# Attention and a two-layer ELU network on one core: the last 40 keys by 64x64 tiles, and a plain second layer in one more group

## The chip, the cores and the metric

The kernel runs on one core of a Trainium2 chip. Its time is the device time of one execution in microseconds (us); the profile is of one such execution. TensorE is PE in the profile (its weight loads are PEld), VectorE is DVE, ScalarE is ACT, GpSimd is POOL, and SyncE is SP, which issues nearly all the transfers.

## The reference

Everything is float32. q, k and v are 4 x 8 x 768 x 64 (batch, heads, positions, width). A query sees the first 8 keys and the 96 keys that end with itself. Scores have a penalty that grows with distance, then a softmax:

```python
scores = q @ k.T / 8 - slope[h] * dist
scores = where((j < 8) | ((0 <= i - j) & (i - j < 96)), scores, -1e9)
a = softmax(scores);  attn = a @ v
x = attn.transpose(0, 2, 1, 3).reshape(3072, 512)
h = x @ w_in                      # 512 x 2048
out = where(h > 0, h, exp(min(h, 0)) - 1) @ w_out    # 2048 x 512
```

## The kernel before

**Groups.** The 3072 rows are 12 groups of 256 (two row tiles of 128), numbered from 0. Each group has 4 pairs of heads for attention, then the two layers, over 16 blocks `fc` of 128 hidden units. A float32 factor is split into two float32r parts (HI and LO), and three of the four part products are summed. Groups 0 to 2 run interleaved, four blocks at a time (`SEGS`), while the 32 weight blocks are loaded and converted from 64-bit floats by ACT, DVE and POOL (`weight`); between segments their partial sums wait in the tiles `pa0` to `pa5` (`part`). The later groups run one after the other.

**Attention of groups 3 to 11.** `visit` number k is one run of TensorE work: the values product of the pair that was visited two before (`values`, line 616), then the scores of a new pair (line 469), in the same two PSUM banks. In between a pair goes through softmax on DVE and ACT (lines 457, 459), a division on POOL (579), a 32x32 transpose on DVE (584) into `tr`, a store to DRAM (`dd<-tr`, 593, two transfers) and a reload that completes the transposition (603): keys 0 to 127 into `pt`, and the last 40 keys into `pu`. `pu` is a constant pair of tiles in which one half of the 128 partitions stays zero; head pairs 0 and 2 use one half, 1 and 3 the other. `values` multiplies `pt` by `v` and `pu` by `u`, each with 8 matmuls in tiles of 128 rows x 64 columns and 64 moving columns; the trace has two records for each matmul. Scores have 8 matmuls in tiles of 64x64, with 168 moving columns. There are 36 pairs and 38 visits.

**Second layer.** `moe` (lines 834 and 860) is plain: per block 12 matmuls of 256 columns for the first layer and 6 of 512 for the second. `seven` (712 and 768) takes two blocks j = (2j, 2j+1) together with 7 products in place of 8: 24 matmuls up and 21 of 256 columns down. It needs sums of weights: `prepare(j)` forms four of them, splits each in HI and LO, stores three in DRAM (`mixed`) and writes the fourth over the right half of the weight block `w0`; each group reloads three per j into `mix` tiles, whose slots are `pa0` to `pa5` again. It also needs sums of activations (`combine`: lines 733 to 736 on DVE, two casts on ACT, two subtractions on DVE). Groups 0 to 2 use `moe`, 3 to 11 `seven` (`NE = 3`).

**Order.** Nothing is scheduled by hand: `Plan.order` simulates the engines with fixed costs, takes what is ready by due time, shares out slots, and writes one fixed order for each engine, SP's queue included. Tiles of one class get slots in the order in which they were asked for. `early` is a moment of the plan before which an operation isn't placed. Line 307 is the shared subtraction and line 299 the shared ACT copy, so they are told apart by tile names.

Of the kernel before, what the change touches and what calls it, by code (L numbers as in the profile page):

```python
# [244 lines left out]
class Kernel:  # L245
# [64 lines left out]
    def consts(self):  # L310
        self.ident = self.const("ident", [P, P])
        self.far0, self.far1 = self.const("far0", [P, LW]), self.const("far1", [P, LW])

        self.scale = self.const("scale", [P, self.NP])
        if self.ON_PE:
            self.minus1 = self.const("minus1", [P, P], F32R)
        self.pu = [self.const(f"pu{i}", [P, 4, 2, NT, 32]) for i in range(2)]
        self.nmax = self.const("nmax", [P, self.B * self.H * self.S // P])
        self.sums = {x: self.c.tile([P, 2 * NT, 4], F32, name=x) for x in self.SLOTS["st"]}

# [238 lines left out]
    def turned(self, b, hp, t0, ss, due, end, X, after):  # L559

        nc, p = self.nc, self.plan
        tr = self.sb("tr", "tr", [P, BLK, 2, NT, 32], slots=X.get("tr"))
        dd = self.dr("dd", "dd", [P * BLK, 2 * NT * 32])
        pt, pu = self.sb("pt4", "pt4", [P, 4, 2, NT, 32], slots=X.get("pt4")), self.pu[hp % 2]
        low = slice(HW, P) if hp % 2 == 0 else slice(0, HW)
        st = self.sum()
        prs = []
        for j in range(2):
            h, at = 2 * hp + j, due + 300 * j
            for i in range(NT):  # L570
                prs.append(self.sb("pr", "pr", [P, BLK * 32], slots=X.get("pr")))
                self.softmax(b, h, t0 + i, ss[j], i, prs[-1], 0, st, NT * j + i, at, after)
        self.inverse(st, 2 * NT, due - 3500, 500.0)
        for n, pr in enumerate(prs):
            j, i = n // NT, n % NT

            def divide(e, n=n, pr=pr):
                nc.gpsimd.memset(pr.t[:, LW:], 0.0)
                nc.gpsimd.tensor_scalar(pr.t[:, :LW], pr.t[:, :LW], st.t[:, n, 3:4], 1.0, ALU.mult, ALU.mult)  # L579

            p.add((("POOL", 160 + 1.1 * LW, True),), divide, [pr, st], [pr], due - 3000 + 10 * n)

            def turn(e, i=i, j=j, pr=pr):
                nc.vector.transpose(tr.t[:, :, j, i], pr.t.rearrange("p (b r) -> p b r", r=32))  # L584

            p.add((("DVE", 150 + 1.042 * 32 * BLK, False),), turn, [pr], [tr], due - 2500 + 10 * n, slack=300.0)
        outs = []
        for a, (w0, w1) in enumerate(((0, 4), (4, BLK))):
            w = w1 - w0
            at = slice(P * w0, P * w1)  # L590

            def out(e, w0=w0, w1=w1, w=w, at=at):
                nc.sync.dma_start(dd.t[at].rearrange("(p w) x -> p (w x)", w=w), tr.t[:, w0:w1].rearrange("p w j i r -> p (w j i r)"))

            outs.append(p.add(sp(), out, [tr], [dd], due - 2000, nbytes=P * w * 512, beside=tuple(outs)))
        for a, (w0, w1) in enumerate(((0, 4), (4, BLK))):
            w = w1 - w0
            rows = slice(0, P) if a == 0 else low
            at = slice(P * w0, P * w1)

            def back(e, x=(pt, pu)[a], w=w, rows=rows, at=at):
                src = dd.t[at].rearrange("(q k w) x -> (k w) q x", q=4, w=w)
                nc.sync.dma_start(x.t[rows].rearrange("k q j i t -> k q (j i t)"), src)

            p.add(sp(), back, [dd], [(pt, pu)[a]], due - 1900, nbytes=P * w * 512)
        return pt, pu

    def values(self, rest, hp, ss):

        pt, pu, v, u = rest  # L610
        v0, v1 = (x.t.rearrange("p (i r j d) -> p i r j d", i=NT, r=2, j=2) for x in (v, u))
        for a, vx, x in ((0, v0, pt), (1, v1, pu)):
            for i in range(NT):
                for r in range(2):
                    for j in range(2):
                        self.nc.tensor.matmul(ss[i].t[j * HW:(j + 1) * HW, r, LW:LW + HW].rearrange("p (c t) -> p c t", c=2), vx[:, i, r, j],  # L616
                                              x.t[:, 2 * r:2 * r + 2, j, i], start=(a, r) == (0, 0), stop=(a, r) == (1, 1))
# [40 lines left out]
    def prepare(self, j, due):  # L658
# [5 lines left out]
        p.add(sp(), lambda e: nc.sync.dma_start(kept.t, w0.t[:, :, right].bitcast(F32)), [w0], [kept], due, nbytes=P * M * 8)  # L664
        self.mixed[j] = {}

        def two(n):
            return dve(n) + pool(n)

        def split(tf, d):  # L670
            p.add(act(M) + pool(M, False), lambda e: self.copy(e, w0.t[:, HI, right], tf.t), [tf], [w0], d)
            p.add(two(M), lambda e: self.minus(e, w0.t[:, LO, right], tf.t, w0.t[:, HI, right]), [tf, w0], [w0], d + 10)

        def stored(n, tf, d):
            split(tf, d)
# [9 lines left out]
        def rest(a, ax, t, tf, d):  # L685
# [12 lines left out]
    def seven(self, rows, xh, xl, dues, step, last):  # L698

# [203 lines left out]
    def build(self):  # L903
# [58 lines left out]
        for x in self.pu:  # L962
            self.plan.add((("POOL", 620.0, True),), lambda e, x=x: self.nc.gpsimd.memset(x.t, 0.0), [], [x], 60000.0, early=50000.0)
# [260 lines left out]
def layouts(q, k, v, w_in, w_out):  # L1224
# [70 lines left out]
```

## Time and profile before

| | |
|---|---|
| Median of 3 runs | 677.93 us (676.97 to 679.39) |
| The profiled execution | 677.09 us, of which the span is 675.3 us |
| TensorE busy in the span | 646.4 us (96%) |
| DVE, ACT, POOL busy | 523.5, 425.5, 188.8 us |
| Granted TensorE clock, mean | 0.997 of 2.4 GHz |

The span runs from the first to the last instruction. The 1.8 us around it are not seen in the trace. A busy share is an average over the three stages that the windows tell apart: three interleaved groups with weight conversion up to about 222 us, the groups by `seven` from there to about 665 us, and the last stores.

### The profile page before, as it was taken

What the parts mean: (1) busy time and instruction counts of PE and PEld (TensorE: products, weight loads), DVE (VectorE), ACT (ScalarE), POOL (GpSimd) and SP (SyncE); (2) the same over time, 40 slices, a digit from 0 to 9 for tenths busy, and PEclk for the clock granted to TensorE, in tenths of its full rate; (3) what the DMA queues carried; (4) which work ended last, traced back from release to release, by engine and by line L of the source; (5) the groups of instructions that cost most, each with busy time, mean ns of one, the idle gap of its engine ahead of it and who ended that gap; (6) DMA issues with size and microseconds to landing.
All of it is one profiled execution on the core that took longest, in us unless ns stands there. A gap on an engine that the chain in (4) does not pass through costs nothing.

```text
span 675.3 us, 18188 instructions
## 1 busy us (share of the span) xinstructions
PE 646.4 (96%) x6534; PEld 594.4 (88%) x6534; DVE 523.5 (78%) x1709; ACT 425.5 (63%) x1217; POOL 188.8 (28%) x477
## 2 busy tenths in 40 slices
PE   8989999968989999999999999999999999999995
PEld 6767887757878899999999999999999999999995
DVE  6999998999976787777777777777777777766654
ACT  6998875556655556666666666666666666655552
POOL 3565575456563332112112112112111111110000
PEclk9999999999999999999999999999999999999998
DMA  8989735110177888788788888788788789775542
GB/s 316 359 303 401 278 120 157 49 62 32 63 228 218 272 279 247 255 261 272 233 265 252 245 263 263 242 265 272 234 266 259 236 261 275 218 228 151 172 141 81
DMA packets 104703, 151.85 MB, mean 225 GB/s; under 512 B 9248, under 2 KB 49952, under 8 KB 104608
## 3 DMA queue, kind: packets, MB, share of 16 engines
q1 hardware_dynamic: 104608, 150.64, 69.8%
q8 instruction: 53, 0.87, 0.5%
q14 instruction: 42, 0.34, 0.2%
HBM read 121.77 MB, written 28.84 MB: 223 GB/s over the span
## 4 chain that ended last, share of the span: by engine, by line
PE 76%; DVE 11%; DMA 5%; issue 2%; ACT 2%; POOL 2%; SPq 1%; DVEq 0%; ACTq 0%; POOLq 0%
PE h L712 27%; PE o L768 24%; PE o L860 5%; PE s L616 5%; PE h L834 5%; PE s L469 4%; DMA mixed<-w 2%; PE pv L502 1%; DVE g L393 1%; PE none L1057 1%; DVE g L395 1%; DVE gl L307 1%; DVE pr L457 1%; DVE w L307 1%; DMA pt<-dd 1%
## 5 line engine op out<-in xcount | busy, mean ns | idle before, releaser
L712 PE MATMUL h<-xh,w 128*128 128x256 f32 x1152 | 160.4, 281 | 1.1 <-DVE gg L722 1.1
L579 POOL TENSOR_SCALAR pr<-pr,st 128x168 f32<-128x168 f32 x144 | 64.6, 449 | 305.8 <-DVE st L477 292.8
L712 PEld LDWEIGHTS h<-xh,w 128*128 128x128 f32 x1152 | 145.3, 188 | 5.4 <-issue 3.3
L722 DVE SCALAR_TENSOR_TENSOR gg<-e,h 128x256 f32<-128x256 f32 x144 | 60.3, 419 | 84.8 <-ACT e L721 83.8
L720 ACT ACTIVATE e<-h 128x256 f32<-128x256 f32 x144 | 55.1, 383 | 75.5 <-PE h L712 75.3
L459 ACT ACTIVATE pr<-pr,nmax 128x168 f32<-128x168 f32 x192 | 82.4, 430 | 16.2 <-DVE nmax L457 15.7
L712 PE MATMUL h<-xl,w 128*128 128x256 f32 x576 | 91.2, 280 | 0.0
L712 PEld LDWEIGHTS h<-xl,w 128*128 128x128 f32 x576 | 77.8, 188 | 0.7 <-issue 0.5
L768 PE MATMUL o<-mix,sh 128*128 128x256 f32 x432 | 74.0, 279 | 0.0
L834 PEld LDWEIGHTS h<-xh,w 128*128 128x128 f32 x384 | 55.9, 188 | 17.5 <-DVE gl L307 9.1
L834 PE MATMUL h<-xh,w 128*128 128x256 f32 x384 | 61.6, 285 | 7.1 <-DVE gl L307 5.8
L457 DVE CUSTOM_DVE_ANT_0 pr<-s,far 128x168 f32<-128x168 f32 x192 | 54.3, 324 | 16.9 <-ACT xh L299 15.2
L860 PE MATMUL o<-w,gh 128*128 128x512 f32 x192 | 61.6, 405 | 3.8 <-DVE part L880 1.8
L299 ACT CAST sh<-sum 128x512 fp32r<-128x512 f32 x72 | 44.8, 622 | 31.9 <-DVE sum L736 31.9
L307 POOL TENSOR_TENSOR w<-g,w 128x256 fp32r<-128x256 f32 x64 | 55.0, 883 | 30.2 <-ACT w L299 24.4
L768 PE MATMUL o<-w,sh 128*128 128x256 f32 x432 | 62.6, 280 | 0.7 <-DVE ob L798 0.7
L721 ACT ACTIVATE e<-e 128x256 f32<-128x256 f32 x144 | 60.1, 417 | 4.1
L768 PEld LDWEIGHTS o<-mix,sh 128*128 128x128 f32 x432 | 61.0, 188 | 0.0
L768 PEld LDWEIGHTS o<-w,sh 128*128 128x128 f32 x432 | 56.0, 188 | 0.7 <-ACT e L720 0.7
L584 DVE STREAM_TRANSPOSE tr<-pr 128x192 f32<-128x192 f32 x144 | 49.1, 361 | 4.7 <-POOL pr L579 2.4
L307 DVE TENSOR_TENSOR sh<-sum,sh 128x512 fp32r<-128x512 f32 x72 | 49.3, 685 | 3.3 <-ACT sh L299 3.3
L299 ACT CAST rh<-gg 128x384 fp32r<-128x384 f32 x72 | 36.8, 511 | 21.8 <-DVE gg L722 21.2
(130 smaller groups left out, 1267.0 us busy)
## 6 DMA issues: line engine op xcount, KB each, us to landing
mix<-mixed SPq DMA_DIRECT2D x216, 256.0 KB, 4.1
qk<-in_qkv_dram SPq DMA_DIRECT2D x48, 312.0 KB, 3.4
v<-in_qkv_dram SPq DMA_DIRECT2D x48, 256.0 KB, 4.1
dd<-tr SPq DMA_DIRECT2D x36, 256.0 KB, 3.5
pt<-dd SPq DMA_DIRECT2D x36, 256.0 KB, 4.4
bits<-in_w_in_dram SPq DMA_DIRECT2D x16, 512.0 KB, 7.4
bits<-in_w_out_dram SPq DMA_DIRECT2D x16, 512.0 KB, 9.0
u<-in_qkv_dram SPq DMA_DIRECT2D x24, 256.0 KB, 4.8
```

The lines of the kernel that those rows point to most:

```text
L299: self.nc.scalar.copy(out, x)
L307: self.on(e).tensor_tensor(out, x, y, ALU.subtract)
L457: first = p.add((("DVE", 85 + 1.042 * LW, False),), lambda e: nc.vector.tensor_tensor_reduce(x(), s.t[:, i, :LW], tab, -(2.0 ** -(h + 1)), ...
L459: p.add(act(LW, extra=200), lambda e: nc.scalar.activation(x(), x(), AF.Exp, bias=nm, scale=-1.0, accum_out=st.t[:, n, 0:1]), [pr], [pr, s ...
L579: nc.gpsimd.tensor_scalar(pr.t[:, :LW], pr.t[:, :LW], st.t[:, n, 3:4], 1.0, ALU.mult, ALU.mult)
L712: nc.tensor.matmul(h.t, w1.t[:, s, cc * P:(cc + 1) * P], x.t[:, cc], start=n == 0 and s == HI and cc == 0, stop=n == 1 and cc == self.NCC - 1)
L720: p.add(act(W, True), lambda e: nc.scalar.activation(ex.t, h.t, AF.Relu, scale=-1.0), [h], [ex], d - 8000)
L721: p.add(act(W), lambda e: nc.scalar.activation(ex.t, ex.t, AF.Exp, scale=-1.0), [ex], [ex], d - 8000)
L722: p.add(dve(W), lambda e: nc.vector.scalar_tensor_tensor(gs(), ex.t, -1.0, h.t, ALU.add, ALU.max), [h, ex], [g], d - 8000)
L768: nc.tensor.matmul(acc[bank].t[:, half], a, b.t[:, LO if t == 1 else HI, x], start=j == 0 and t == 0 and n in first, stop=j == self.NFC // ...
L834: nc.tensor.matmul(h.t, w1.t[:, s, cc * P:(cc + 1) * P], x.t[:, cc], start=n == 0 and cc == 0, stop=n == 2 and cc == self.NCC - 1)
L860: nc.tensor.matmul(o.t[:, :at.stop - at.start], g.t[:, i * P:(i + 1) * P], w2.t[:, s, at], start=fc == f0 and n == 0 and s == HI, stop=fc ...
```

## The change

It has two parts.

**The last 40 keys.** `pu` holds one row tile in partitions 0 to 63 and the other in 64 to 127, without zeros, in two ordinary slots; `u` holds the values for both kinds of head pair. Its 8 matmuls become 8 of 64x64 tiles, four tiles in turn. `tr` and `pt` have the row tile ahead of the head, and `pu` is filled by two transfers (64 partitions, 256-byte pieces) where there was one (512-byte pieces).

**Group 3 by `moe`.** `SE = 4` is the first group by `seven`. `prepare` is planned beside group 3 rather than beside groups 0 to 2, not before 165 us of the plan; the three stored sums are split into `mix` tiles of their own rather than in place over `w0`, and only the fourth is written over `w0`. Slots are added: `gl` 3 (2 before), `tf` 4 (2), `hl` 2 (1).

```diff
-        self.pu = [self.const(f"pu{i}", [P, 4, 2, NT, 32]) for i in range(2)]
...
-        tr = self.sb("tr", "tr", [P, BLK, 2, NT, 32], slots=X.get("tr"))
+        tr = self.sb("tr", "tr", [P, BLK, NT, 2, 32], slots=X.get("tr"))
-        pt, pu = self.sb("pt4", "pt4", [P, 4, 2, NT, 32], slots=X.get("pt4")), self.pu[hp % 2]
-        low = slice(HW, P) if hp % 2 == 0 else slice(0, HW)
+        pt, pu = self.sb("pt4", "pt4", [P, 4, NT, 2, 32], slots=X.get("pt4")), self.sb("pu", "pu", [P, 4, 2, 32])
...
-            p.add(sp(), back, [dd], [(pt, pu)[a]], due - 1900, nbytes=P * w * 512)
+        p.add(sp(), back, [dd], [pt], due - 1900, nbytes=P * 2048)
+        backs = []
+        for i in range(NT):
+            def back(e, i=i):
+                src = dd.t[P * 4:].rearrange("(q k w) x -> (k w) q x", q=4, w=2)[:, :, i * HW:(i + 1) * HW]
+                nc.sync.dma_start(pu.t[i * HW:(i + 1) * HW].rearrange("k q j t -> k q (j t)"), src)
+
+            backs.append(p.add(sp(), back, [dd], [pu], due - 1890, nbytes=P * 512, beside=tuple(backs)))
...
+        for r in range(2):
+            for j in range(2):
+                for i in range(NT):
+                    rows = slice(i * HW, (i + 1) * HW)
+                    self.nc.tensor.matmul(out(i, r, j), ux[rows, hp % 2, r, j], pu.t[rows, 2 * r:2 * r + 2, j], start=False, stop=r == 1)
...
-            cost += 720.0
+            cost += 660.0
...
         def stored(n, tf, d):
-            split(tf, d)
+            x = self.sb("mix", "mix", [P, 2, M], F32R)
+            split(tf, x, left, d)
...
-        t1 = less(w0, right, w0, left, due)
-        t = less(w1, right, w0, right, due)
-        stored(3, t, due + 100)
-        rest(w1, right, t1, t, due + 200)
-        stored(2, t, due + 200)
-        rest(w1, left, t, t, due + 300)
-        stored(4, t, due + 300)
-        split(t1, due + 400)
+        t3, t1 = less(w1, right, w0, right, due), less(w0, right, w0, left, due + 50)
+        stored(3, t3, due + 100)
+        split(t1, w0, right, due + 200)
+        t2 = rest(w1, right, t1, due + 150)
+        stored(2, t2, due + 200)
+        stored(4, rest(w1, left, t2, due + 250), due + 300)
...
-                if n >= self.NE:
+                if n >= self.SE:
...
-            d = max(x[2 * j + 1] for (n, f0, f1), x in zip(segs, dues) if n < self.NE and 2 * j + 1 in x) + self.PREPARE[0]
-            todo.append((min(start[self.NE] - 1.0, d), lambda j=j, d=d: self.prepare(j, d)))
+            d = [x for (n, _, _), x in zip(segs, dues) if n == self.SE - 1][-1][2 * j + 1] + self.PREPARE[0]
+            todo.append((start[self.SE] - 1.0, lambda j=j, d=d: self.prepare(j, d)))
...
-    PREPARE = (9000.0,)
+    PREPARE, SE = (6000.0, 165000.0), 4
```

## Rows read from the trace of the kernel before

**Rows 1.** The page, busy us, share and instructions of each engine.

```profile
PE 646.4 (96%) x6534; PEld 594.4 (88%) x6534; DVE 523.5 (78%) x1709; ACT 425.5 (63%) x1217; POOL 188.8 (28%) x477
```

**Rows 2.** Windows: stretch, length, busy us of each engine, clock, DMA share, GB/s.

```profile
60.00:100.00 40.00, 40.00 (x362) 34.28 (x359) 37.41 (x93) 32.38 (x89) 25.63 (x38) 1.00 0.65 233
100.00:120.00 20.00, 18.89 (x149) 15.34 (x148) 18.23 (x46) 11.63 (x34) 11.80 (x21) 1.00 0.50 148
120.00:195.00 75.00, 65.81 (x438) 55.55 (x437) 73.62 (x163) 46.24 (x120) 44.16 (x59) 1.00 0.20 68
135.00:165.00 30.00, 21.93 (x128) 17.52 (x127) 29.27 (x54) 16.40 (x38) 17.37 (x21) 1.00 0.13 44
195.00:262.00 67.00, 62.97 (x667) 56.90 (x666) 48.65 (x168) 34.76 (x111) 24.23 (x69) 1.00 0.81 253
262.00:615.00 353.00, 352.59 (x3844) 340.51 (x3843) 257.67 (x932) 223.78 (x642) 51.64 (x216) 1.00 0.82 252
```

**Rows 3.** Waits of PE in 120 to 195 us, the longest: total, times, longest.

```profile
PE h L834 <- DVE gl L307: 4.9, 3, 3.4
```

**Rows 4.** DVE groups, 135 to 165 us: `prepare`, first and last of six.

```profile
L307 DVE TENSOR_TENSOR w<-tf,w 128x256 fp32r<-128x256 f32 x5 | 2.7, 532 | 0.0
...
L307 DVE TENSOR_TENSOR tf<-w,tf 128x256 f32<-128x256 f32 x2 | 0.8, 412 | 0.0
```

**Rows 5.** PE timeline of one visit: start us, length us, record counts.

```profile
347.89 0.69 PE L616 MATMUL s<-pt,v 128*64 128x64 f32 x16
348.41 0.64 PE L616 MATMUL s<-pu,u 128*64 128x64 f32 x16
348.98 0.80 PE L469 MATMUL s<-qk 64*64 64x168 f32 x16
349.71 0.74 PE L768 MATMUL o<-w,rh 128*128 128x256 f32 x4
```

**Rows 6.** PE group of the `pu` records, 262 to 615 us.

```profile
L616 PE MATMUL s<-pu,u 128*64 128x64 f32 x448 | 18.0, 223 | 0.0
```

**Rows 7.** Chain in order of time: start us, us, what.

```profile
121.11 1.17 PE o L860 x5
...
292.35 2.47 PE o L768 x21
```

**Rows 8.** SP timeline and PE timeline around the visit at 511 us.

```profile
505.37 0.58 SPq L603 DMA_DIRECT2D pu<-dd  x1
...
510.64 0.69 PE L616 MATMUL s<-pt,v 128*64 128x64 f32 x16
511.29 0.69 PE L616 MATMUL s<-pu,u 128*64 128x64 f32 x16
511.91 0.80 PE L469 MATMUL s<-qk 64*64 64x168 f32 x16
```

**Rows 9.** Tile `pu`: transfers to landing, all 36.

```profile
DMA to landing us min/median/max: 2.9/4.6/6.4
```

**Rows 10.** DVE groups, whole span: `prepare`, first and last of six.

```profile
L307 DVE TENSOR_TENSOR w<-tf,w 128x256 fp32r<-128x256 f32 x24 | 12.1, 502 | 6.7 <-POOL w L301 6.0 <-ACT w L299 0.7
...
L682 DVE TENSOR_TENSOR tf<-hl 128x256 f32<-128x256 f32 x10 | 5.8, 581 | 0.6 <-POOL w L307 0.6
```

**Rows 11.** DVE groups, whole span: what `combine` and the plain layer need.

```profile
L307 DVE TENSOR_TENSOR sh<-sum,sh 128x512 fp32r<-128x512 f32 x72 | 49.3, 685 | 3.3 <-ACT sh L299 3.3
L307 DVE TENSOR_TENSOR rl<-gg,rh 128x384 fp32r<-128x384 f32 x72 | 39.2, 544 | 1.2 <-ACT rh L299 1.2
L736 DVE TENSOR_TENSOR sum<-gg,sum 128x128 f32<-128x128 f32 x72 | 21.7, 301 | 2.5
L307 DVE TENSOR_TENSOR gl<-h,gh 128x256 fp32r<-128x256 f32 x48 | 19.9, 414 | 2.1 <-ACT gh L299 1.9
```

**Rows 12.** DVE groups, 195 to 262 us: `prepare`, first and last of six.

```profile
L307 DVE TENSOR_TENSOR w<-tf,w 128x256 fp32r<-128x256 f32 x6 | 2.5, 422 | 5.7 <-POOL w L301 5.7
...
L682 DVE TENSOR_TENSOR tf<-hl 128x256 f32<-128x256 f32 x1 | 0.5, 450 | 0.6 <-POOL w L307 0.6
```

More of the change, by code (lines that the diff above doesn't have):

```diff
@@ L583, in turn @@
             def turn(e, i=i, j=j, pr=pr):
-                nc.vector.transpose(tr.t[:, :, j, i], pr.t.rearrange("p (b r) -> p b r", r=32))
+                nc.vector.transpose(tr.t[:, :, i, j], pr.t.rearrange("p (b r) -> p b r", r=32))
             p.add((("DVE", 150 + 1.042 * 32 * BLK, False),), turn, [pr], [tr], due - 2500 + 10 * n, slack=300.0)
@@ L592, in out, with back @@
             def out(e, w0=w0, w1=w1, w=w, at=at):
-                nc.sync.dma_start(dd.t[at].rearrange("(p w) x -> p (w x)", w=w), tr.t[:, w0:w1].rearrange("p w j i r -> p (w j i r)"))
+                nc.sync.dma_start(dd.t[at].rearrange("(p w) x -> p (w x)", w=w), tr.t[:, w0:w1].rearrange("p w i j r -> p (w i j r)"))
             outs.append(p.add(sp(), out, [tr], [dd], due - 2000, nbytes=P * w * 512, beside=tuple(outs)))
[L596 to L603, printed above, removed]
-            p.add(sp(), back, [dd], [(pt, pu)[a]], due - 1900, nbytes=P * w * 512)
+        def back(e):
+            src = dd.t[:P * 4].rearrange("(q k w) x -> (k w) q x", q=4, w=4)
+            nc.sync.dma_start(pt.t.rearrange("k q i j t -> k q (i j t)"), src)
+        p.add(sp(), back, [dd], [pt], due - 1900, nbytes=P * 2048)
[5 more added lines that the diff above has]
+            backs.append(p.add(sp(), back, [dd], [pu], due - 1890, nbytes=P * 512, beside=tuple(backs)))
         return pt, pu
@@ L610, in values @@
         pt, pu, v, u = rest
[L611 to L617, printed above, removed]
+        vx = v.t.rearrange("p (i r j d) -> p i r j d", i=NT, r=2, j=2)
+        ux = u.t.rearrange("p (m r j d) -> p m r j d", m=2, r=2, j=2)
+        out = lambda i, r, j: ss[i].t[j * HW:(j + 1) * HW, r, LW:LW + HW].rearrange("p (c t) -> p c t", c=2)
+        for i in range(NT):
+            for r in range(2):
+                for j in range(2):
+                    self.nc.tensor.matmul(out(i, r, j), vx[:, i, r, j], pt.t[:, 2 * r:2 * r + 2, i, j], start=r == 0, stop=False)
+        for r in range(2):
+            for j in range(2):
+                for i in range(NT):
+                    rows = slice(i * HW, (i + 1) * HW)
+                    self.nc.tensor.matmul(out(i, r, j), ux[rows, hp % 2, r, j], pu.t[rows, 2 * r:2 * r + 2, j], start=False, stop=r == 1)
     def visit(self, k, due):
@@ L663, in prepare @@
         self.kept[j] = kept = self.dr(f"kept{j}", "kept", [P, 2, M])
-        p.add(sp(), lambda e: nc.sync.dma_start(kept.t, w0.t[:, :, right].bitcast(F32)), [w0], [kept], due, nbytes=P * M * 8)
+        p.add(sp(), lambda e: nc.sync.dma_start(kept.t, w0.t[:, :, right].bitcast(F32)), [w0], [kept], due, nbytes=P * M * 8, early=self.PREPARE[1])
         self.mixed[j] = {}
@@ L668, in two, with split @@
             return dve(n) + pool(n)
-        def split(tf, d):
-            p.add(act(M) + pool(M, False), lambda e: self.copy(e, w0.t[:, HI, right], tf.t), [tf], [w0], d)
-            p.add(two(M), lambda e: self.minus(e, w0.t[:, LO, right], tf.t, w0.t[:, HI, right]), [tf, w0], [w0], d + 10)
+        def split(tf, x, at, d):
+            p.add(act(M) + pool(M, False), lambda e: self.copy(e, x.t[:, HI, at], tf.t), [tf], [x], d)
+            p.add(two(M), lambda e: self.minus(e, x.t[:, LO, at], tf.t, x.t[:, HI, at]), [tf, x], [x], d + 10)
@@ L674, in stored @@
         def stored(n, tf, d):
-            split(tf, d)
+            x = self.sb("mix", "mix", [P, 2, M], F32R)
+            split(tf, x, left, d)
             s = self.mixed[j][n] = self.dr(f"mix{j}{n}", "mixed", [P, 2, M])
-            p.add(sp(), lambda e: nc.sync.dma_start(s.t, w0.t[:, :, right].bitcast(F32)), [w0], [s], d + 30, nbytes=P * M * 8)
+            p.add(sp(), lambda e: nc.sync.dma_start(s.t, x.t.bitcast(F32)), [x], [s], d + 30, nbytes=P * M * 8)
         def less(a, ax, b, bx, d):
@@ L680, in less, with rest @@
             hl, tf = self.sb("hl", "hl", [P, 2, M]), self.sb("tf", "tf", [P, M])
-            p.add(two(2 * M), lambda e: self.minus(e, hl.t, a.t[:, :, ax], b.t[:, :, bx]), [a, b], [hl], d)
+            p.add(two(2 * M), lambda e: self.minus(e, hl.t, a.t[:, :, ax], b.t[:, :, bx]), [a, b], [hl], d, early=self.PREPARE[1])
             p.add(two(M), lambda e: self.on(e).tensor_tensor(tf.t, hl.t[:, HI], hl.t[:, LO], ALU.add), [hl], [tf], d + 1)
             return tf
-        def rest(a, ax, t, tf, d):
+        def rest(a, ax, t, d):
+            tf = self.sb("tf", "tf", [P, M])
@@ L686, in rest @@
             p.add(two(M), lambda e: self.minus(e, tf.t, a.t[:, HI, ax], t.t), [a, t], [tf], d)
             p.add(two(M), lambda e: self.on(e).tensor_tensor(tf.t, tf.t, a.t[:, LO, ax], ALU.add), [a, tf], [tf], d + 1)
[L689 to L696 removed]
+            return tf
@@ L961, in build @@
         self.kept, self.mixed = {}, {}
-        for x in self.pu:
-            self.plan.add((("POOL", 620.0, True),), lambda e, x=x: self.nc.gpsimd.memset(x.t, 0.0), [], [x], 60000.0, early=50000.0)
         for j in range(NFC // 2):
-            d = max(x[2 * j + 1] for (n, f0, f1), x in zip(segs, dues) if n < self.NE and 2 * j + 1 in x) + self.PREPARE[0]
-            todo.append((min(start[self.NE] - 1.0, d), lambda j=j, d=d: self.prepare(j, d)))
+            d = [x for (n, _, _), x in zip(segs, dues) if n == self.SE - 1][-1][2 * j + 1] + self.PREPARE[0]
+            todo.append((start[self.SE] - 1.0, lambda j=j, d=d: self.prepare(j, d)))
         for _, f in sorted(todo, key=lambda x: x[0]):
@@ L996 @@
              "x": ["x0"], "xh": ["xh0", "xh1", "xh2"], "xl": ["xl0", "xl1", "xl2"], "e": ["e0", "e1"], "gh": ["gh0", "gh1", "gh2"],
-             "gl": ["gl0", "gl1"], "io": ["io0", "io1", "io2", "io3"], "part": [f"pa{i}" for i in range(6)], "mix": [f"pa{i}" for i in range(6)], "hl": ["x0"], "tf": ["tf0", "tf1"],
+             "gl": ["gl0", "gl1", "gl2"], "io": ["io0", "io1", "io2", "io3"], "part": [f"pa{i}" for i in range(6)], "mix": [f"pa{i}" for i in range(6)], "pu": ["pu0", "pu1"], "hl": ["x0", "ph2"], "tf": ["tf0", "tf1", "tf2", "tf3"],
              "g": ["io2", "io3"], "sum7": ["ph2", "x0"], "rh": ["gh0", "gh1"], "rl": ["gl0", "gl1"], "sh": ["xh2", "xl2"], "o2": ["v0"], "o3": ["t0"]}
@@ L1253, in layouts @@
     first = at % 4 * 32 + at // 4
-    vp = np.zeros_like(vv)
-    vp[..., 0, :, :, :, :] = vv[:, :, :, first, 0]
     key = at % 2 * 32 + at % HW // 2
+    vp = vv[..., :NT, :, :, :][:, :, :, first].copy()
+    vp[:, :, :, :, 0] = vv[:, :, :, first, 0]
     for m in range(2):
-        rows = slice((1 - m) * HW, (2 - m) * HW)
         x = np.zeros_like(vv[:, :, ::2, :HW, 1])
         x[:, :, :, :LW - P] = vv[:, :, ::2, (2 - m) * HW - (LW - P):(2 - m) * HW, 1]
-        vp[:, :, ::2, rows, 1] = x[:, :, :, key[:HW]]
+        x = x[:, :, :, key[:HW]]
+        for i in range(NT):
+            vp[:, :, ::2, i * HW:(i + 1) * HW, 1, m] = x[:, :, :, :, i]
     halves = lambda x: x.reshape(B, nb, H // 2, D, 2, -1).swapaxes(3, 4).reshape(B, nb, H // 2, 2 * D, -1)
```

## The prediction

> **What bounds the kernel now.** I read the page's busy line first: TensorE has 646.4 us of 675.3 busy [rows 1], so only two things can move the end, TensorE's work and its 29 us of idle time. The windows by stage then say where the idle time lies [rows 2]. From 262 to 615 us PE is busy for 352.59 of 353 us: there a microsecond of matmuls removed is a microsecond gained, and relief of any other engine is worth nothing. From 60 to 100 us it is busy throughout as well, with DVE at 37.41 of 40. But from 100 to 120 it idles 20 - 18.89 = 1.1 us and from 120 to 195 it idles 75 - 65.81 = 9.2 us, of which 8.1 lie in 135 to 165. DVE is busy there for 73.62 of 75 us. The DMA share of 0.20 excludes transfers as the limit. From 195 to 262 PE idles 4.0 us with DVE at 48.65 of 67 (73%).
>
> The waits name the engine of the middle stretch [rows 3]: the first layer's matmuls wait for `gl`, the last product of the DVE chain that frees the PSUM bank, for 4.9 us in three pieces. What keeps DVE from it: in 135 to 165 us, beside the conversion of weights, it makes the sums of `prepare`, six groups from 2.7 us down to 0.8, together 10.8 us of the 29.27 that it works there [rows 4].
>
> **The visits.** In one visit the 16 `pt` records take 348.41 - 347.89 = 0.52 us, the 16 `pu` records 0.57 and the 16 scores records 0.73 [rows 5]. Per record, scores have 168 columns and the others 64. In columns over time that is 1024 / 0.57 = 1.8 per ns with two tiles side by side and 2688 / 0.73 = 3.7 per ns with four. So the four tiles of 64x64 do stream together, and about twice as fast. The new `pu` block uses the same four tiles in the same turn. Its price lies between 0.57 us (if its records are bound by their number and not by their columns: 0.57 / 16 = 36 ns each, and scores' 46 ns each doesn't exclude that) and 1024 / 3.7 = 0.28. Some of each block is the change of tile shape ahead of the next, and one such change stays; a block that begins afresh, at 511.29, takes 0.62 instead of 0.57 [rows 8]. I allow 0.10 us for the change of shape, an estimate, and halve the remaining 0.47: 0.23 us saved per visit, ends 0 and 0.29. The number of changes of shape stays the same wherever scores follow the values: the change from 128x64 to 64x64 moves ahead of `pu`, and none is left ahead of scores.
>
> Behind 262 us, where PE is full, 448 `pu` records are 28 visits [rows 6]: 28 x 0.23 = 6.5 us (0 to 8.1). The other 8 of the 36 lie in stages with idle time; of their 1.9 us I count half, 0.9 (0 to 2.3).
>
> The Trainium skill (TensorEngine Tiling (Array Packing), Performance Considerations) speaks against this: a matmul has about 60 cycles of overhead, and no tiling factor is to be taken from a dimension that is already small, as 64 columns are. At 2.4 GHz 60 cycles are 25 ns, so 16 records would by it not go under 0.40 us, and the saving would be near 0.1 us in place of 0.23. No row of before shows it, since no block has four tiles and 64 columns.
>
> **The second transfer for `pu`.** SP issues `pu` in 0.58 us [rows 8]. A second issue moves what is queued behind it on SP (the next `u`, `v` and `mix` loads) by as much, and the second half lands some 0.6 us later than today's whole. SP mostly waits for PE in that stage, so its queue has room. The landing has little: issued at 505.37 with a median of 4.6 us to land and a maximum of 6.4 [rows 9], `pu` was just in time or late for 511.29. That block began 0.65 us after `pt` in place of 0.52, a wait of 0.13. If two visits of each of the 7 groups behind 262 lost the whole 0.6 us, it would cost 8.4 us; but the planner counts the second issue too and puts other matmuls ahead of a visit whose data it thinks late. I take 0.6 us in all, ends 0 and 8.4.
>
> **Group 3 by `moe`.** Behind the first stage PE's pace is its matmul rate. 5 records of 512 columns take 1.17 us, 21 of 256 columns 2.47 [rows 7]. Two blocks of the plain second layer are 12 records, 12 x 0.234 = 2.81 us, against 2.46 by `seven`: 0.35 more, eight times, +2.8 us. The first layer is the same in both. This is certain as long as PE is full.
>
> On DVE the group gets lighter. Beside the ELU, which both have, `seven` needs for two blocks `sh` 0.685, `rl` 0.544 and four sums of up to 0.30, together 2.4 us; the plain layer needs two `gl` of 0.414, 0.8 [rows 11]. Eight times 1.6 is 12.8 us less.
>
> **`prepare` moves.** All of it on DVE is 44.1 us in six groups from 12.1 down to 5.8 [rows 10]. 7.6 us of that lie in 195 to 262 already [rows 12], so up to 36 us leave the time before 195. With them gone, DVE's need in 120 to 195 falls well under PE's, conversion of the late weights ends earlier, and what is left is a stage like 60 to 100 us, in which PE lost nothing. Of the 10.3 us of idle time in 100 to 195 I leave 2: -8.3 us. Bounds: -10.3 (all of it), 0 (something else holds the weights, which no row suggests).
>
> The price is paid behind it. In the counterpart of 195 to 262 DVE's need becomes 48.65 - 7.6 - 12.8 + 44.1 = 72.4 us in 67 + 2.8, 104%. But the 44.1 were worked in a crowded stage: the costliest group has a mean of 0.502 us over the span [rows 10] and 0.422 in 195 to 262 [rows 12]. Scaled by 0.84 they are 37, and the sum is 65, 94%. POOL, at 24.23 of 67, can take some, and a little of `prepare` fits ahead of it. 94% with PE full is what 60 to 100 us shows; 98% with 12% of PE's time lost is what 120 to 195 shows. So the stretch's idle time may be 2 us or 8 instead of 4; I take 5, +1.0.
>
> A wait is added: the 24 stored sums take their `mix` slots ahead of group 4's first reload, since the class is served in order. Whatever `prepare` is late then holds PE at group 4's first second layer, at about 250 us, and everything behind it.
>
> **The sum.** -6.5 - 0.9 + 0.6 + 2.8 - 8.3 + 1.0 = -11.3 us on an execution of 677.1 us, so 665.8. The median shown is 0.8 above this execution; the prediction for a median is 666.6.
>
> **Rivals.**
> (1) The stall moves. DVE at 98% of the `prepare` stretch costs PE 12% of 67 us, 8.2 in place of 5, and some late weights still hold PE up (6 us left in place of 2): +7.2, 673.8. For it: 120 to 195. Against it: the third `gl` slot, and that the 12.8 us of `combine` are gone.
> (2) Four tiles don't pay at 64 columns, because each record has its price: -7.4 and no more, 674.0. For it: no row with this shape. Against it: scores at 3.7 columns per ns. This is the skill's rule driven to its end; by the rule itself, with 0.1 us left per visit, it would be 670.
> (3) Slower. `prepare` isn't through when group 4 needs its first sums. DVE's idle time in 195 to 262 is 18.4 us; with 12.8 + 7.6 released it is 38.8, 5.3 short of 44.1 without any help. If the durations are stretched by a third more, to 58, it is 20 short, and PE stands nearly that long at about 250 us. It decides from 13.4 us of lateness on; at 17 the time is 683. For it: the ordered slots, and that `part` holds them until groups 0 to 2 end. Against it: POOL's room, and lower clean durations.
> (4) The `pu` half lands too late in most visits, +6: 672.6. For it: the 0.13 us at 511.29. Against it: the planner's order.
>
> **How the numbers follow.** Main case 0.55 (662 to 671), (1) 0.17, (2) 0.08, (3) 0.10, (4) 0.10. The range takes the main case, and (1), (2) and (4) up to 674.5: 660 to 674.5, low end from the bounds -8.1, -1.5, +2.8, -10.3 and 0. A measurement here tells no less than 0.3% (2 us). Faster: all of the main case and nearly all of (1), (2) and (4), 0.86; same 0.04; slower 0.10.
>
> **What would show it.** `pu` records in tiles 64*64, with about 0.25 to 0.3 us to the scores, and visits near 1.58 us instead of 1.82. No `prepare` in DVE's groups before 150 us; PE full from 60 to about 185. Lines 834 and 860 in group 3, and no line 768 before about 250. DVE at about 90% from 185 to 250, and no wait of TensorE for `mix` at group 4's first second layer: that wait would make the forecast wrong. So would `pu` blocks of 0.4 us or more, or waits for `pu<-dd` in every group.

## The result, and the profile after

The changed kernel takes 659.45 us (median of 4 executions, 658.65 to 663.09) against 677.92 us for the kernel before beside it: a ratio of 0.9732 (95% interval 0.9696 to 0.9768), 18.5 us less. Timed once more it took 658.81 us (median of 5, 657.95 to 660.02), ratio 0.9726 (0.9697 to 0.9756). Forecast were 666.6 us, in a range of 660.0 to 674.5: the direction was right, the gain was 7 us too small.

The profiled execution was the slowest of the first four, 663.09 us with a span of 661.2. The busy line of its page, beside [rows 1]:

```profile
PE 641.3 (97%) x6462; PEld 587.2 (89%) x6462; DVE 504.0 (76%) x1658; ACT 419.0 (63%) x1211; POOL 199.0 (30%) x494
```

The same line of the second profiled execution, 658.23 us with a span of 656.4, which is nearer to the median:

```profile
PE 638.0 (97%) x6462; PEld 585.0 (89%) x6462; DVE 504.6 (77%) x1658; ACT 419.5 (64%) x1211; POOL 200.1 (30%) x494
```

From [rows 1] to this one TensorE's busy time falls by 646.4 - 638.0 = 8.4 us and its idle time by 28.9 - 18.4 = 10.5 us. The windows of the first profile, with the columns of [rows 2], say where:

```profile
60.00:100.00 40.00, 39.51 (x359) 33.57 (x358) 34.05 (x105) 33.19 (x98) 19.51 (x38) 1.00 0.62 219
100.00:120.00 20.00, 19.86 (x164) 17.30 (x163) 17.95 (x31) 12.43 (x30) 11.26 (x16) 1.00 0.36 115
120.00:195.00 75.00, 73.63 (x541) 64.70 (x540) 63.79 (x157) 46.29 (x127) 41.81 (x66) 1.00 0.22 70
135.00:165.00 30.00, 30.00 (x191) 26.52 (x190) 25.18 (x52) 18.95 (x44) 14.13 (x19) 1.00 0.03 10
195.00:262.00 67.00, 63.72 (x576) 54.16 (x575) 54.30 (x168) 36.43 (x121) 44.20 (x93) 0.97 0.71 233
262.00:615.00 353.00, 350.66 (x3870) 337.87 (x3869) 257.57 (x930) 223.07 (x637) 52.74 (x213) 1.00 0.81 247
```

In 120 to 195 us TensorE now idles for 1.4 us (9.2 before) and DVE works 63.79 of 75 (73.62 before). The 30 us that had 8.1 us of idle time are full. In 195 to 262 the idle time is 3.3 us (4.0 before), though the weight sums are made there now. The waits of TensorE in that stretch (total, times, longest):

```profile
PE o L866 <- ACT gh L299: 2.7, 2, 1.6
PE h L840 <- DVE gl L307: 0.6, 2, 0.4
```

TensorE waits nowhere for `mix`. The first product of `seven` (line 774 now) starts at 268.9 us. One visit in TensorE's timeline, beside [rows 5]:

```profile
369.29 0.69 PE L617 MATMUL s<-pt,v 128*64 128x64 f32 x16
369.90 0.46 PE L622 MATMUL s<-pu,u 64*64 64x64 f32 x16
370.19 0.75 PE L468 MATMUL s<-qk 64*64 64x168 f32 x16
370.87 0.50 PE L774 MATMUL o<-w,rh 128*128 128x256 f32 x2
```

From the start of one block to the next: `pt` 0.61 us (0.52 before), `pu` 0.29 (0.57), scores 0.68 (0.73), together 1.58 us instead of 1.82.

### The profile page after: what moved, and what is told of

The parts are those of the page before. It is cut to its first block, busy times and chain, and to the rows that moved or that the text cites. A ratio compares the mean times of both kernels' runs of the same rounds, so it can differ in the third digit from the quotient of the medians.

```text
span 661.2 us, 17979 instructions
## 1 busy us (share of the span) xinstructions
PE 641.3 (97%) x6462; PEld 587.2 (89%) x6462; DVE 504.0 (76%) x1658; ACT 419.0 (63%) x1211; POOL 199.0 (30%) x494
## 4 chain that ended last, share of the span: by engine, by line
PE 81%; DVE 10%; ACT 3%; POOL 3%; issue 2%; DMA 1%; SPq 0%; DVEq 0%; POOLq 0%; ACTq 0%
PE h L718 27%; PE o L774 23%; PE o L866 10%; PE h L840 9%; PE s L468 3%; PE s L617 3%; PE s L622 2%; PE none L1061 1%; DVE pr L456 1%; PE pv L501 1%; DMA pu<-dd 1%; ACT pr L458 1%; DVE g L394 1%; DVE gl L307 1%; PE t L521 1%
## 5 line engine op out<-in xcount | busy, mean ns | idle before, releaser
L728 DVE SCALAR_TENSOR_TENSOR gg<-e,h 128x256 f32<-128x256 f32 x128 | 53.6, 419 | 76.8 <-ACT e L727 76.0
L866 PE MATMUL o<-w,gh 128*128 128x512 f32 x256 | 82.5, 406 | 3.4 <-ACT gh L299 3.1
L718 PE MATMUL h<-xl,w 128*128 128x256 f32 x512 | 81.2, 280 | 0.0
L718 PEld LDWEIGHTS h<-xl,w 128*128 128x128 f32 x512 | 69.2, 188 | 0.9 <-issue 0.7
L456 DVE CUSTOM_DVE_ANT_0 pr<-s,far 128x168 f32<-128x168 f32 x192 | 54.3, 324 | 18.5 <-ACT xh L299 13.7
L774 PE MATMUL o<-mix,sh 128*128 128x256 f32 x384 | 65.8, 279 | 0.0
L774 PE MATMUL o<-w,sh 128*128 128x256 f32 x384 | 55.7, 280 | 0.7 <-DVE ob L804 0.7
L727 ACT ACTIVATE e<-e 128x256 f32<-128x256 f32 x128 | 53.4, 417 | 3.6
L866 PEld LDWEIGHTS o<-w,gh 128*128 128x128 f32 x256 | 43.7, 191 | 12.1 <-ACT gh L299 5.4
L774 PEld LDWEIGHTS o<-mix,sh 128*128 128x128 f32 x384 | 54.2, 189 | 0.0
L774 PEld LDWEIGHTS o<-w,sh 128*128 128x128 f32 x384 | 49.8, 189 | 0.7 <-ACT e L726 0.7
```

The lines of the kernel that those rows point to most:

```text
L456: first = p.add((("DVE", 85 + 1.042 * LW, False),), lambda e: nc.vector.tensor_tensor_reduce(x(), s.t[:, i, :LW], tab, -(2.0 ** -(h + 1)), ...
L718: nc.tensor.matmul(h.t, w1.t[:, s, cc * P:(cc + 1) * P], x.t[:, cc], start=n == 0 and s == HI and cc == 0, stop=n == 1 and cc == self.NCC - 1)
L727: p.add(act(W), lambda e: nc.scalar.activation(ex.t, ex.t, AF.Exp, scale=-1.0), [ex], [ex], d - 8000)
L728: p.add(dve(W), lambda e: nc.vector.scalar_tensor_tensor(gs(), ex.t, -1.0, h.t, ALU.add, ALU.max), [h, ex], [g], d - 8000)
L774: nc.tensor.matmul(acc[bank].t[:, half], a, b.t[:, LO if t == 1 else HI, x], start=j == 0 and t == 0 and n in first, stop=j == self.NFC // ...
L866: nc.tensor.matmul(o.t[:, :at.stop - at.start], g.t[:, i * P:(i + 1) * P], w2.t[:, s, at], start=fc == f0 and n == 0 and s == HI, stop=fc ...
```

## The experiments

**Each part by itself.** Two kernels, each with one half of the change: the tiles alone (the hunks of `turned`, `values` and the planner's cost 660, with the two `pu` slots), and the plain layer alone (`prepare` in its new form, `SE = 4`, and the slots of `gl`, `hl` and `tf`, with three of `tf`).

```diff
# tiles_only, on the kernel before
-        pt, pu = self.sb("pt4", "pt4", [P, 4, 2, NT, 32], slots=X.get("pt4")), self.pu[hp % 2]
+        pt, pu = self.sb("pt4", "pt4", [P, 4, NT, 2, 32], slots=X.get("pt4")), self.sb("pu", "pu", [P, 4, 2, 32])
...
# plain_only, on the kernel before
-                if n >= self.NE:
+                if n >= self.SE:
...
-    PREPARE = (9000.0,)
+    PREPARE, SE = (6000.0, 165000.0), 4
```

> Only the 64x64 tiles and the two transfers for pu; group 3 still by seven, sums where they were. My theory (the parts add up; 36 visits x 0.234 = 8.4 us of matmuls less, of which the 28 behind 262 us count in full, less some waiting for the later half of pu): 670 to 672.5. Rival (shorter visits relieve the first stage too, so this part carries the gain that my sum lacked): 662 to 666. Rival (the gain per visit is lost in waits): 676 to 678.

> Only group 3 by the plain layer with the sums moved beside it; pu is as before, and the scratch class tf has 3 slots and not 4, for room. My theory: 12 to 14 us less idle time ahead of 262 us, against 2.8 us more matmuls and a little idle time beside group 3: 665.5 to 669. Rival (the moved sums stall group 3 as much as they had stalled the first stage): 676 to 681. The parts add up if this gain and that of the tiles alone together make 18.5 us.

The tiles alone took 667.67 us, ratio 0.9858 (0.9825 to 0.9892), 9.6 us less than before. The plain layer alone took 667.09 us, 0.9848 (0.9818 to 0.9878), 10.2 less. The tiles alone took less than the 670 to 672.5 us that I expected and more than the first rival's 662 to 666; the plain layer came out as expected. The sum of the two is 19.8, the whole change gave 18.5: the parts add up within their intervals, so nothing shows that one lives on the other. The windows of the tiles alone, where the sums are still beside the first groups:

```profile
120.00:195.00 75.00, 66.94 (x423) 56.58 (x422) 70.54 (x151) 44.09 (x113) 40.99 (x56) 0.93 0.19 65
...
262.00:615.00 353.00, 353.00 (x3904) 340.98 (x3903) 262.32 (x947) 226.60 (x646) 51.63 (x216) 1.00 0.82 256
```

The first stage keeps 8.1 us of idle time (9.2 before), in an execution whose granted clock is 0.93 there and not 1.00, and the later stage is full with two transfers for `pu` in it. The plain layer alone fills the first stage and pays behind it:

```profile
120.00:195.00 75.00, 74.20 (x579) 65.43 (x578) 62.30 (x162) 44.76 (x125) 37.54 (x66) 1.00 0.26 84
195.00:262.00 67.00, 63.56 (x541) 54.47 (x541) 51.92 (x160) 36.18 (x120) 44.96 (x87) 1.00 0.64 209
```

**Why the `pu` block is short.** The program gives the two row halves in turn. If they stream together because of that, the two row tiles one after the other should cost about what two tiles did.

```diff
# rows_in_turn, on the changed kernel
-        for r in range(2):
-            for j in range(2):
-                for i in range(NT):
+        for i in range(NT):
+            for r in range(2):
+                for j in range(2):
```

> The changed kernel with the loop over the row tile outermost in the pu block: the same 16 records of 64x64 tiles, but only two tiles take turns at a time. If four tiles streaming together make the gain, the block goes back from 0.28 to 0.5 or more us, the visit from 1.58 to 1.81, and the time is 659.5 + 7.0 = 666.5 (665 to 668). If it is that half the rows are gone, or that each record has its price, the order doesn't matter: 659.5.

It took 659.55 us, ratio 0.9734 (0.9704 to 0.9765): the same as the changed kernel. TensorE's timeline of one of its visits:

```profile
365.86 0.69 PE L617 MATMUL s<-pt,v 128*64 128x64 f32 x16
366.47 0.47 PE L622 MATMUL s<-pu,u 64*64 64x64 f32 x16
366.76 0.77 PE L468 MATMUL s<-qk 64*64 64x168 f32 x16
367.45 0.50 PE L774 MATMUL o<-w,rh 128*128 128x256 f32 x2
```

The `pu` block is 0.29 us again. So my reason, the turn in the program's order, fell; the gain does not hang on it. The run would fit two other reasons: that both row halves are used in the block, or that 64 rows are cheaper than 128. The kernel before has blocks of the same shape on one row half alone, in the attention of group 2:

```profile
67.35 0.68 PE L502 MATMUL pv<-pt,u 64*64 64x64 f32 x16
67.97 0.73 PE L860 MATMUL o<-w,gh 128*128 128x512 f32 x2
```

There 16 records take 0.62 us with the change of shape behind them, so 64 rows alone do not make a block short, and the use of both halves is what stays. That is a comparison of two kinds of block and not of one edit; `pu` with both row tiles on one half was not tried.

**What the weight sums cost before.** The kernel before, and the changed kernel, with the sums left out: the same number of stores, of the weights as they are. The waits between the sums and their stores go with them.

```diff
# before_no_sums, on the kernel before; after_no_sums likewise on the changed one, with early=self.PREPARE[1]
-        t1 = less(w0, right, w0, left, due)
-        t = less(w1, right, w0, right, due)
-        stored(3, t, due + 100)
...
+        for n in (3, 2, 4):
+            s = self.mixed[j][n] = self.dr(f"mix{j}{n}", "mixed", [P, 2, M])
+            p.add(sp(), lambda e, s=s: nc.sync.dma_start(s.t, w1.t[:, :, right].bitcast(F32)), [w1], [s], due + 30 + 100 * n, nbytes=P * M * 8, early=100000.0)
```

> The kernel before, without the sums and splits of prepare: the three stored blocks are copies of a weight block as it is, with the same size and number of transfers, from 100 us of the plan on. My theory (DVE, crowded by prepare, held the first stage): PE's idle time in 100 to 195 us falls from 10.3 to under 2, and the time to 664.5 to 668. Rival (conversion of the late weights alone fills DVE, or their transfers): 10 us of idle time stay, 675 to 678.

> The changed kernel, without the sums and splits of prepare in the same way. It gives what the moved sums still cost beside group 3. My theory (DVE is at 81% there and POOL at 66%, and PE idled 3.3 us in 195 to 262 and 1.3 in 262 to 315): 655 to 657.5. Rival (they are hidden, and those waits are attention's): 658.5 to 660.

Without sums the kernel before took 658.95 us, ratio 0.9735 (0.97 to 0.9771): 18.1 us less, where the step of the forecast had at most 10.3, and below the 664.5 to 668 us that I expected of this run. The page's busy line of this kernel:

```profile
PE 642.0 (98%) x6534; PEld 595.5 (91%) x6534; DVE 488.5 (74%) x1646; ACT 417.4 (64%) x1194; POOL 154.7 (24%) x435
```

And three of its windows:

```profile
100.00:120.00 20.00, 20.00 (x164) 17.66 (x163) 17.30 (x37) 12.34 (x30) 11.34 (x22) 1.00 0.75 240
120.00:195.00 75.00, 74.25 (x580) 65.67 (x580) 54.04 (x142) 45.07 (x124) 27.93 (x54) 1.00 0.36 115
195.00:262.00 67.00, 67.00 (x705) 63.79 (x704) 50.41 (x178) 40.19 (x119) 11.99 (x44) 1.00 0.80 252
```

Two things are to be seen. The 4.0 us of idle time in 195 to 262 of before, which the forecast had kept, are gone too: they belonged to the sums. And the same 6534 records of TensorE are busy for 642.0 us instead of 646.4 [rows 1]. TensorE's work is the same, so 4.4 us of what looked like work were lost time. Idle time 28.9 to 15.0 is 13.9 us; 13.9 + 4.4 = 18.3 us agree with the 18.1 between the medians.

What this run does not tell apart is the arithmetic of the sums and their order. In the kernel before the four sums of one j are split in place over the right half of `w0`, one after the other, so that a split waits until the store ahead of it has landed; without sums these waits are gone too. In 195 to 262 us of the kernel before, POOL waits for such stores (total, times, longest):

```profile
POOL w L301 <- DMA mixed<-w: 18.2, 6, 4.6
```

In 120 to 195 us the same wait is 3.1 us, and DVE has only 1.4 us without work [rows 2], so there DVE's load is the nearer reason. For the 4.0 us behind 195 the wait in place is a rival that no run tests.

The changed kernel without sums took 666.54 us, ratio 0.9849 (0.9819 to 0.9878), 7 us more than with them. Its longest wait of TensorE (total, times, longest):

```profile
PE s L617 <- DMA pt<-dd: 11.1, 2, 10.4
```

Three rows of its SP timeline (start, length, what, how many):

```profile
188.62 1.37 SPq L591 DMA_DIRECT2D dd<-tr  x2
...
194.17 1.94 SPq L673 DMA_DIRECT2D mixed<-w  x3
...
203.38 0.43 SPq L596 DMA_DIRECT2D pt<-dd  x1
```

With no arithmetic to wait for, 19 of the 32 stores (24 `mixed`, and 8 `kept`, which save the right half of `w0`) were issued between 180 and 201 us of SP's queue, mostly at 0.5 to 0.7 us each. Ten of them, beside other transfers, stand between a pair's store to `dd` and its reload, and TensorE waited for `pt` for 10.4 us in one piece. Neither expectation held. The run says nothing of the sums beside group 3: it made a stall of its own. The next one takes its place.

**What the sums cost after.** The arithmetic of the sums is taken out, their stores stay at their places: two copies on ACT fill each tile that is stored.

```diff
# copies_for_sums, on the changed kernel
-        def split(tf, x, at, d):
-            p.add(act(M) + pool(M, False), lambda e: self.copy(e, x.t[:, HI, at], tf.t), [tf], [x], d)
-            p.add(two(M), lambda e: self.minus(e, x.t[:, LO, at], tf.t, x.t[:, HI, at]), [tf, x], [x], d + 10)
+        def split(x, at, d):
+            p.add(act(M), lambda e: self.copy(e, x.t[:, HI, at], w1.t[:, HI, right]), [w1], [x], d)
+            p.add(act(M), lambda e: self.copy(e, x.t[:, LO, at], w1.t[:, LO, right]), [w1], [x], d + 10)
```

> The changed kernel with the moved sums' VectorE and GpSimd work left out: each split is two copies of a weight block on ScalarE, stored through the same tiles at the same point of the plan, so that the transfers keep their pace. My theory (beside group 3 the sums crowd DVE, and PE still loses about 5 us there): idle time of PE in 195 to 262 us from 3.3 to under 1.5, time 652.5 to 656. Rival (that loss is attention's, or a granted clock that falls): 658 to 660.

It took 654.05 us, ratio 0.9648 (0.9625 to 0.9672): 5 us below the changed kernel, as expected. Its window beside group 3:

```profile
195.00:262.00 67.00, 65.70 (x572) 57.47 (x571) 34.56 (x130) 46.60 (x153) 9.76 (x43) 1.00 0.65 212
```

DVE is at 34.56 us there, POOL at 9.76: some 20 us of DVE and 34 of POOL less than in that stretch of the changed kernel. So the sums cost 18.1 us where they stood, waits in place included, and about 5 where they stand now. The 5 are a net figure, since the copies load ACT there with 46.60 us instead of 36.43.

**What the plain group costs.** The kernel before without sums, and group 3 by `moe` in it. What neither kernel pays for is out of both.

```diff
# no_sums_plain, on before_no_sums
-                if n >= self.NE:
+                if n >= self.NE + 1:
```

> The kernel before without the sums, as measured at 659.0, and with group 3 by the plain layer. It prices the plain layer alone, with no crowding in either kernel. My theory (48 units of 256 columns at 0.117 us, with PE full): 2.8 us more, 661 to 662.5. Rival (the lighter DVE work of the plain layer gives it back): 658.5 to 659.5.

It took 662.97 us (659.23 to 664.04), ratio 0.9768 (0.9737 to 0.9799): by the medians 4.0 us above the kernel without sums, by the two ratios, each to the kernel before timed beside it, 2.2. Forecast were 2.8, and the run does not tell these apart. Less 8.4 us for 36 shorter visits it would be 654.6, near the 654.05 of the copies, which supports the 5 us. In 195 to 262 TensorE is full:

```profile
195.00:262.00 67.00, 67.00 (x585) 59.14 (x582) 34.31 (x129) 36.33 (x117) 10.64 (x48) 1.00 0.52 161
```

**Other places for the sums.** If beside group 3 they cost 5 us, another group by `moe` or another start might take some of that away.

```diff
# one_more_plain; sums_earlier; sums_later; sums_later_due_later, on the changed kernel
-    PREPARE, SE = (6000.0, 165000.0), 4
+    PREPARE, SE = (6000.0, 165000.0), 5
...
+    PREPARE, SE = (6000.0, 140000.0), 4
...
+    PREPARE, SE = (6000.0, 185000.0), 4
...
+    PREPARE, SE = (12000.0, 185000.0), 4
```

> The changed kernel with groups 3 and 4 by the plain layer and the sums made beside both. If the sums cost 5 us beside one group and little when spread over two, the 2.8 us of the second plain group are earned back: 656.5 to 658.5. If not: 661 to 662.5.

> The changed kernel with the sums allowed from 140 us of the plan on instead of 165. The parts that need no stored tile may then start beside the last weight blocks. If DVE has room there (it was busy for 64 of 75 us in 120 to 195), group 3 is relieved: 657 to 658.5. If the crowding just returns: 660 to 664.

> The changed kernel with the sums allowed from 185 us of the plan on instead of 165; due times as they are. Sums from 140 on cost 5 us more, with PE's idle time in 120 to 262 us 4 us higher. If that is crowding of DVE ahead of group 3's start, later is no worse: 657 to 660, with 74.5 or more of 75 us of PE busy in 120 to 195. If the room ahead of group 3 is needed for the sums, idle time beside group 3 grows: 661 to 664.

> As the other, and each block's sums due 6 us later (12 behind the block's place in group 3), so that DVE takes the ELU chains and attention first. If what PE loses beside group 3 is a matter of which of two ready operations DVE takes first: 655.5 to 658. If the stored sums then come too late for group 4: a wait of PE for mix at about 255 us and 660 or more.

One more plain group took 659.82 us, ratio 0.9733 (0.9706 to 0.976): the same as the changed kernel, and between the two times that I expected. Its idle time went along with the sums: 195 to 262 is full, and the stretch behind it is not. The window of 195 to 262:

```profile
195.00:262.00 67.00, 67.00 (x576) 59.15 (x576) 35.07 (x131) 37.63 (x120) 12.68 (x50) 1.00 0.50 156
```

The one behind it:

```profile
262.00:315.00 53.00, 49.71 (x461) 42.00 (x460) 42.66 (x130) 29.36 (x98) 37.68 (x72) 1.00 0.66 216
```

From 140 us the kernel took 664.0 us, ratio 0.9798 (0.9764 to 0.9832), some 5 us more, so the crowding returned; from 185 us 660.67, 0.9764 (0.9736 to 0.9792), between the two expectations; due later as well 662.64, 0.9776 (0.9744 to 0.9807), with no wait of TensorE for `mix`, so my theory of the order on DVE fell and the sums were not late either. The windows of the start at 140 us:

```profile
120.00:195.00 75.00, 72.39 (x527) 62.33 (x525) 63.00 (x153) 43.23 (x118) 38.55 (x60) 1.00 0.20 67
195.00:262.00 67.00, 60.93 (x564) 51.47 (x565) 56.04 (x170) 36.80 (x125) 44.70 (x93) 1.00 0.69 222
```

Those of the start at 185 us with the due time as it was:

```profile
120.00:195.00 75.00, 75.00 (x589) 66.11 (x588) 59.23 (x158) 46.81 (x129) 32.96 (x60) 1.00 0.23 70
195.00:262.00 67.00, 60.91 (x518) 49.95 (x517) 56.12 (x165) 34.15 (x116) 52.67 (x98) 1.00 0.76 253
```

Earlier, both stretches lose; later, the first is full and the second loses 6.1 us instead of 3.3. None of these is faster than the changed kernel. Of all runs only `copies_for_sums` is, which leaves the sums' arithmetic out.

## Why the prediction was right and wrong

**The step that failed** is "Of the 10.3 us of idle time in 100 to 195 I leave 2: -8.3 us", with its bound "-10.3 (all of it)". The place was right: the idle time of 100 to 195 fell to 0.14 + 1.37 = 1.5 us, nearly the 2 that I left. The size was wrong, because I measured what the sums cost by TensorE's idle time in that stretch. Taken out, with the waits that they bring, they give back 18.1 us. The two parts that I had not counted are the 4.0 us behind 195, which I kept in the sum, and the 4.4 us that stood in the busy column. How the latter come about is argued, not shown: a record overlaps those behind it (records of 0.28 us follow each other at 2.47 / 21 = 0.12 [rows 7]), and does so less where they come in pieces.

**The price behind it** was put at +1.0, idle time of 4.0 going to 5. Measured from a stretch without sums, which loses nothing, it is about 5 us. From the measured costs of the sums this part is then -18.1 + 5 + 2.8 = -10.3, against -10.2 for this part by itself; with 2.2 or 4.0 for the plain group it would be -10.9 or -9.1. In the forecast it was -8.3 + 1.0 + 2.8 = -4.5. The difference to -10.2 is 5.7 of the 7 us; the visits (1.0, if all 36 count in full) and the second transfer (0.6) are the rest.

**The low end of the range** was not added from the ends of its terms. The eight other visits had an end of -2.3 and the price behind an end of -2.0 (2 us of idle time instead of 4), where the sum took -1.5 and 0. With these ends and 0.8 for a median it would have been 658.0, and 659.45 would have lain inside by width alone, with the cost of the sums still wrong.

**DVE's load there** I put at 65 of 67 + 2.8 us, with "POOL ... can take some". It is 54.30 of 67 (81%). Of the sums, DVE has seven groups in 195 to 262, from 6.1 us down to 1.6, together 24.6 us; POOL has eight, together 32.8. The first and last of DVE's groups (columns as in [rows 4]):

```profile
L307 DVE TENSOR_TENSOR mix<-tf,mix 128x256 fp32r<-128x256 f32 x10 | 6.1, 616 | 1.4 <-ACT mix L299 0.8 <-POOL mix L301 0.6
...
L307 DVE TENSOR_TENSOR hl<-w 128x512 f32<-128x512 f32 x2 | 1.6, 805 | 0.0
```

And POOL's group of the shared subtraction:

```profile
L307 POOL TENSOR_TENSOR mix<-tf,mix 128x256 fp32r<-128x256 f32 x8 | 6.4, 799 | 1.6 <-ACT mix L299 1.3
```

The planner gave POOL about half of them, and I had left POOL's 24.23 of 67 us as a remark and not put it into the sum. The durations did not fall to 0.84 of those of before either, as I had scaled them: a mean of 0.616 us for the shared subtraction, against 0.502 and 0.422 in [rows 10, 12]. The median is 0.424 both before and after; the mean is raised by a few that take up to 1.5 us.

**The visits.** Forecast 1.58 us per visit and 0.25 to 0.3 for the `pu` block; measured 1.58 and 0.28 to 0.29. The change of shape that moves ahead of `pu` shows as 0.09 to 0.10 us more for `pt`, the value that I had allowed. I counted 28 visits in full and 8 by half, -7.4; all 36 at 0.234 are -8.4. The part by itself gave -9.6, with an interval of 7.3 to 11.9 us that holds both, so that the discounted visits count in full is likely and not shown.

**A price for each record (rival 2)** is out: 16 records in 0.29 us are 18 ns each, half of the 36 ns that a full price would have been. The Trainium skill's rule (TensorEngine Tiling (Array Packing), Performance Considerations) of some 60 cycles of overhead for each matmul, with no factor taken from a small dimension, would have given no less than 0.40 us for these 16 records at 2.4 GHz, by the estimate in the prediction. The trace does not agree at 64 columns with four tiles, if each record counts as a matmul; by the program's 8 matmuls the same estimate would be 0.20 us, and 0.29 does not speak against it.

**The second transfer** cost nothing that shows: 353.00 of 353 us are busy with the tiles alone, where I had +0.6 with an end at 8.4. In the changed kernel the rows of `pu` say that the 72 halves land no later than the 36 wholes did [rows 9]:

```profile
DMA to landing us min/median/max: 2.4/3.9/6.4
```

The block waited for `pu<-dd` once, for 0.2 us. Rival 4 is out.

**The late sums (rival 3)** did not come: no wait for `mix` at the first `seven` group. Its sum counted DVE's idle time alone; that POOL took what would have been late is argued from its 32.8 us. Of rival 1, the stall that moves, the direction is right: 5 us of the 18 went along with the sums, and with one more plain group TensorE's idle time moved on with the sums to the next stretch.

**The whole balance.** Sums out of the first stage -18.1, sums beside group 3 +5, plain group +2.8 (2.2 to 4.0), visits -8.4: -18.7 (-19.3 to -17.5), against -18.5 measured.

**Signs.** The first sum on DVE starts at 173.9 us, behind 150 as said; TensorE is busy for 123.52 of 125 us from 60 to 185, nearly full; line 774 starts behind 250; the visits are as said; DVE beside group 3 is at 81% and not at about 90.

Open are the price of the plain group between 2.2 and 4.0 us, what part of the 18.1 us was the sums' arithmetic and what part their waits in place, and the 1.2 us by which the tiles alone gave more than 36 visits explain.

## What to carry to other kernels

Idle time that is read from one stretch of the engine that bounds the kernel need not be all that another engine's work costs it: here 10.3 us were read and 18.1 came back, and what told it was a run that left the work out with its transfers kept. Such a run takes out the waits inside that work too, and does not price them apart. When work is moved, count every engine that the planner may give it to: POOL took 32.8 us of the sums here, beside DVE's 24.6. A run that leaves work out must keep the timing of what is left: ten stores that nothing delayed any more stood ahead of one reload in the same queue, and TensorE waited 10.4 us for it.

## What the runs showed of the hardware

**Row halves ran side by side in both orders that were tried.** With four matmuls of one row half given ahead of four of the other, the block took 0.29 us as with the halves in turn, where a block on one half takes 0.62 with the change of shape. That the halves overlap is read from these blocks; no run puts `pu` on one half.

**The granted clock dipped in some executions.** Four windows of the changed kernel's first profile (columns as in [rows 2]):

```profile
42.00:48.00 6.00, 4.34 (x66) 3.38 (x65) 5.96 (x17) 5.16 (x18) 3.10 (x4) 1.00 1.02 406
48.00:54.00 6.00, 5.78 (x59) 4.31 (x59) 5.25 (x20) 4.35 (x15) 2.21 (x4) 0.72 1.04 410
...
240.00:246.00 6.00, 4.56 (x25) 3.05 (x23) 5.96 (x18) 3.45 (x14) 4.44 (x7) 1.00 0.97 304
246.00:252.00 6.00, 5.73 (x65) 4.92 (x66) 4.54 (x15) 2.80 (x8) 4.84 (x12) 0.72 0.55 201
```

TensorE idled for 1.4 to 1.7 us of 6, and in the 6 us behind that the mean clock is 0.72, a mixture of the levels of 2.4 and 1.2 GHz: 0.28 x 6 = 1.7 us lost each time, 3.4 together, as an estimate. The second execution had the same pause ahead of 48 us and no dip there, and one dip later, where I had expected none:

```profile
42.00:48.00 6.00, 4.12 (x64) 3.23 (x62) 5.97 (x20) 5.17 (x18) 3.80 (x6) 1.00 1.02 404
48.00:54.00 6.00, 6.00 (x69) 5.31 (x67) 5.77 (x21) 5.54 (x18) 2.14 (x3) 1.00 1.04 414
...
240.00:246.00 6.00, 4.49 (x22) 3.44 (x21) 5.93 (x17) 4.00 (x15) 5.56 (x13) 0.83 0.71 222
246.00:252.00 6.00, 6.00 (x74) 5.11 (x73) 4.34 (x18) 3.25 (x12) 2.92 (x6) 0.89 0.72 237
```

That is (0.17 + 0.11) x 6 = 1.7 us. So by this estimate the clock makes up 1.7 of the 4.9 us between the two executions; one with the first one's mean clock, 0.994, took 659.07 us. What else made the first one long stays open.

In the kernel before the clock stays at 1.00 in 135 to 165 us with TensorE busy for 21.93 of 30 [rows 2]; with the tiles alone it is 0.83 in the same stretch, at 23.33 of 30:

```profile
135.00:165.00 30.00, 23.33 (x117) 19.17 (x116) 27.09 (x51) 15.79 (x36) 15.58 (x19) 0.83 0.13 45
```

Which pauses bring the lower level and which do not, these rows don't tell.
